# Lightning attention into a leaky-ReLU MLP on one core: another order of the first entries, and plan constants set for it

## Chip, core and metric

The kernel runs on one core of one Trainium2 chip. The metric is the device time of one execution in microseconds (us).

## What is computed

Block-wise linear attention with decay, for 4 batches, 8 heads, 768 tokens and head size 64, then a two-layer MLP on the 3072 tokens, all in float32 (the two weights arrive as float64).

```python
# attention, per block of 64 tokens; lam is one decay per head
intra = (q_b @ k_b^T * Dmask) @ v_b          # Dmask[i,j] = lam**(i-j) for i >= j
inter = (q_b * lam**(pos+1)) @ kv_state
out_b = intra + inter
kv_state = lam**64 * kv_state + (k_b * lam**(63-pos))^T @ v_b
# MLP: x is (3072, 512), w_in (512, 2048), w_out (2048, 512)
h = x @ w_in
out = maximum(0.01 * h, h) @ w_out
```

## The kernel before

**Tiles.** Tokens are worked in 24 chunks of 128 (c0 to c23; six to a batch, two blocks to a chunk) and 6 groups of four chunks. `w_in` is cut into 8 pairs of 256 columns each. To keep float32 accuracy on TensorE each operand is split into a head h, a low part l and a mixed part m; a product is three passes, xh·wh, xl·wl and xm·wm. Between the second and third pass ACT scales the PSUM bank (L658); after the third ACT applies the leaky ReLU and moves the bank out (L661, "evacuation"), and a DMA stores the result g to DRAM (L664).

**Entries.** The list `seq` names the work of the first two groups by hand: `a` (a whole chunk alone), `b` (load and transpose two chunks, scores of the first), `r` c (a chunk round: outputs of c, scores of c+1, transposes of c+2, loads of c+2), `wi` p (load and convert pair p of `w_in`), `up` g p (a unit: group g times pair p, or a part of its chunks), `ls`/`lt` (loads of many small pieces for later chunks). Later groups follow from a loop, and the second layer (`dl`, `dn`) comes at the end.

**The plan.** Each entry calls `add` with an engine, a cost, what it reads and writes, and the rank of its entry. `Plan.emit` runs a list schedule over those costs and issues the instructions in that order, so the order on each engine is fixed when the program is built: every engine works its own list strictly in turn. SP issues nearly all DMAs. A `busy` transposition (L266) fills gaps that the plan expects on PE.

**What a chunk does.** k and q (L338, two DMAs each) and v (L388) are loaded. PE transposes k and q (L403); for the first four chunks k goes to bank b11 (`KT`) and later to the upper half of `po`, q always goes to `pt`. ACT copies both to SBUF (L414 for k, L415 for q). POOL, or DVE for c < KM, scales k (L419). The q times powers of lambda (L423) is made by DVE straight from `pt` for c < QS, and else by POOL. PE makes scores and key-value products into `psc` (L313); DVE takes them out (L452 masked scores, L457/L459 state), POOL decays the state (L462). PE makes outputs into `po` (L313): own products, first inter products, then, after a tiny copy `seen_po` on ACT or DVE (L491), the second inter products. ACT writes xh (L507), DVE xl (L508) and xm (L510).

**What a weight pair does.** For each half: a load of float64 words into one of three `raw` buffers (L566, a "raw"), on ACT two conversions into `low` (L580, L582) and one into `w32` (L578), on DVE a shift and an add (L584, L585). Then the head wh on ACT or DVE (L591, L593), wl (L596) and wm (L602) on DVE. The three raw buffers, two `low` buffers and `w32` are used in turn by all pairs.

**Banks of the units.** Each unit has two blocks with a bank each. The first `EARLY` blocks alternate between b10 and b2; after that b10, b11 and b2 go round.

```python
kb = ("b10", "b2")[n_b % 2] if n_b < 0 else ("b10", "b11", "b2")[n_b % 3]   # n_b starts at -EARLY
```

**Constants that the change sets.** `LATER` is added to the rank of xm of the first group. `GOFIRST`: below it the scores of a chunk are issued before its key-value products. `SUBL`, `RUNS` and the costs in `load_kq` and `load_v` are costs and due times of loads in the plan. `SOON` is a table of latencies used for the fillers.

Of the kernel before, what the change touches and what calls it, by code (L numbers as in the profile page):

```python
# [31 lines left out]
def _bc(ap, idx, n):  # L32
    a = [list(x) for x in ap.ap]
    return bass.AP(ap.tensor, ap.offset, a[:idx] + [[0, n]] + a[idx:])


class Plan:

    LAG = {"PE": 0.25, "ACT": 0.1, "DVE": 0.1, "POOL": 0.12, "DMA": 3.5}
    SOON = dict(LAG, DMA=2.0)

    def __init__(self):
        self.ops, self.last, self.rank = [], {}, 0.0
# [36 lines left out]
    def emit(self):  # L83
        n = len(self.ops)
        follows, heads = {}, {}
        for c in self.chains.values():
            m = [i for i in c if "PE" in self.ops[i][0]]
            for i in c[1:]:
                self.ops[m[0]][2].update(self.ops[i][2] - set(c))
            heads[m[0]] = m[1:]  # L90
            follows.update((i, m[0]) for i in m[1:])
        locked = []
        left = [len(o[2]) for o in self.ops]
        users = [[] for _ in range(n)]
        for i, o in enumerate(self.ops):
            for d in o[2]:
                users[d].append(i)
        free = dict(self.first)
        ends = [[] for _ in range(n)]
        able = {e: set() for e in free}  # L100
        for i, o in enumerate(self.ops):
            if not left[i]:
                for e in o[0]:
                    able[e].add(i)

        def since(i, e):
            return max((t + (0.0 if e == x != "DMA" else self.LAG[x]) for t, x in ends[i]), default=0.0)

        def good(i, e, t):
            ways = self.ops[i][0]  # L110
            return all(t + ways[e] <= max(free[x], t) + ways[x] + 0.3 for x in ways)

        done = []
        while len(done) < n:
            best = None
            for e in free:
                for i in able[e]:
                    if e == "PE" and (i != locked[0] if locked else i in follows):
                        continue
                    t = max(free[e], since(i, e))  # L120
                    if (best is None or (t, self.ops[i][3]) < best[:2]) and good(i, e, t):
                        best = (t, self.ops[i][3], i, e)
            t, _, i, e = best
            ways, fn = self.ops[i][:2]
            if i in heads:
                locked = list(heads[i])
            elif locked and i == locked[0]:
                locked.pop(0)
            for x in ways:
                able[x].discard(i)  # L130
            us = ways[e]
            if e == "PE" and t < self.cold:
                us *= 1.5
            elif e == "DVE" and fn is not None and free["POOL"] > t:
                us += 0.4 * min(free["POOL"] - t, us)
            free[e] = t + us
            done.append((t, len(done), i, e))
            for u in users[i]:
                ends[u].append((free[e] + self.more.get(i, 0.0), e))
                left[u] -= 1  # L140
                if not left[u]:
                    for x in self.ops[u][0]:
                        able[x].add(u)
        self.timeline = sorted(done)

        soon = dict.fromkeys(free, 0.0)
        soon.update(PE=self.warm, DVE=self.first["DVE"], DMA=self.first["DMA"])
        over = [(0.0, None)] * n
        for t, _, i, e in self.timeline:
            ways, fn, deps = self.ops[i][:3]  # L150
            t = max([soon[e]] + [over[d][0] + (0.0 if over[d][1] == e != "DMA" else self.SOON[over[d][1]]) for d in deps])
            if e == "PE":
                if self.spare in self.ops[i][4]:
                    self.idle = None
                if self.idle is not None and t > soon[e] + 0.4:
                    self.idle(int((t - soon[e] - 0.2) / 0.22))
            soon[e] = t + ways[e]
            over[i] = (soon[e], e)
            fn() if len(ways) == 1 else fn(e)
# [3 lines left out]
def kernel(  # L163
# [10 lines left out]
    nc = tc.nc  # L174
    P = 128
    B, H, SEQ, D = q.shape
    C, C2 = P, P // 2
# [7 lines left out]
    NG = NCH // GC  # L185
    T = GC * C
    WARM = 11
    LATER = 5.0
    KT, EARLY = "b11", 2
    QS = 3  # L190
    KM = 1
    NRAW = 3
    TURN = 3
    SLACK, GSLACK = 4.0, 2.0
    EARLY_SLACK = 1.5
    GOFIRST = 2
    SUBL, FIRST = 0.75, -8.0

    DV = 10
    RUNS = {10: (-8.0, 0.8), 12: (4.0, 0.0)}  # L200
    C4 = P // 4
    HALF = (slice(0, D), slice(D, 2 * D))
    assert NCB % TURN == 0 and D == 64 and KO == HP == 4 and SEQ % C == 0 and NCH % GC == 0 and d_model == T == 512 and NP % 4 == 0
# [43 lines left out]
    kqv = [[x[:, i * H * D:(i + 1) * H * D].rearrange("p (h d) -> p h d", h=H) for i in range(2)] for x in kqv_f]  # L247
# [27 lines left out]
    def length(us, issue=0.5):  # L275

        return issue if steady else us

    def move(us, fn, reads, writes, issue=0.5, rank=0.0, slack=SLACK):

        plan.slack = slack if steady else EARLY_SLACK
        if steady and not rank:
            rank = FIRST
        add("DMA", length(us, issue), fn, reads, writes, rank=rank)
        plan.slack = 0.0
# [40 lines left out]
    def of(c):  # L326
        return c // NCB, c % NCB, c % 2
# [3 lines left out]
    def load_kq(c):  # L331
        b, n, i = of(c)
        for src, x, nm in ((k, 0, "k"), (q, 1, "q")):
            y, dst = src[b, :, n * C:(n + 1) * C, :], kqv[x][i]

            def go(y=y, dst=dst):
                for z in range(2):
                    nc.sync.dma_start(out=dst[:, z * HP:(z + 1) * HP, :], in_=y[z::2].rearrange("h p d -> p h d"))  # L338
            if nm == "k" or c < DV:
                move(1.15, go, [], [f"{nm}{i}"], issue=1.0)  # L340

    def run(c):

# [19 lines left out]
    def load_subs(c):  # L363
        b, n, i = of(c)
        count = run(c)[1]
        for nm, src, pieces in zip("kq", (k, q), subs(c, count)):
            for sub, lo, hi, keys in pieces:
                add("DVE", 0.0, lambda: None, [], keys)
                for y in range(lo, hi):
                    for a in range(4):  # L370
# [4 lines left out]
                                out=o.rearrange("j (m i) -> j m i", i=C4), in_=z.rearrange("(m j) i -> j m i", j=C4)),  # L375
                            keys, [f"{nm}s{y}{a}"], issue=SUBL, rank=RUNS.get(c, (4.0, 0.4))[0] + RUNS.get(c, (4.0, 0.4))[1] * (4 * y + a))

# [7 lines left out]

    def load_v(c):
        b, n, i = of(c)
        move(1.15, lambda: nc.sync.dma_start(out=kqv[2][i], in_=v[b, :, n * C:(n + 1) * C, :].rearrange("h p d -> p h d")),  # L388
            [], [f"v{i}"])

    def transposes(c):
# [17 lines left out]
        def copies():  # L409
# [3 lines left out]
            if c < DV:  # L413
# [3 lines left out]
            nr = slice(0, C2 if n == NCB - 1 else P)  # L417
            add(*((("DVE", "POOL"), (0.7, 1.1)) if c < KM else ("POOL", 1.1)),
                lambda e="POOL": ENG[e].tensor_tensor(kr[nr], kr[nr], _bc(pow_k, 3, D)[nr], op=ALU.mult), ["fk"], [f"k{i}"])  # L419
            m = slice(1 if n == 0 else 0, 2)  # L420
            o, x = (z.rearrange("p y (t i) -> p y t i", t=2)[:, :, m, :] for z in (qsTs[i], pt if c < QS else qTs[i]))
            eng, e, us, dep = ("DVE", nc.vector, 0.7, "pt") if c < QS else ("POOL", nc.gpsimd, 1.2, f"qT{i}")
            add(eng, us, lambda: e.tensor_tensor(o, x, _bc(pow_q, 2, 2)[:, :, m, :], op=ALU.mult), ["fq", dep], [f"qsT{i}"])  # L423
# [3 lines left out]
    def scores(c):  # L427
# [16 lines left out]

        if c < GOFIRST:
            add("PE", 0.47, go, [f"kT{i}", f"qT{i}"], ["psc"])
        add("PE", 0.47, kv, [f"k{i}", f"v{i}"], ["psc"])
        if c >= GOFIRST:
            add("PE", 0.47, go, [f"kT{i}", f"qT{i}"], ["psc"])
# [17 lines left out]
    def outputs(c, between=lambda: None):  # L467
# [38 lines left out]
        def uses():  # L506
# [3 lines left out]
            add("DVE", 0.7, lambda: nc.vector.scalar_tensor_tensor(xm, xl.bitcast(F32), -S, xh.bitcast(F32), op0=ALU.mult, op1=ALU.add),  # L510
                [h, l], [m], rank=LATER if c < GC else 0.0)

        return uses

    def alone(c):
        load_kq(c)
        load_v(c)
        transposes(c)()
        scores(c)()
        outputs(c)()  # L520

    def begun(c):

        for x in (c, c + 1):
            load_kq(x)
            load_v(x)
            transposes(x)()
        scores(c)()
# [159 lines left out]
    def down(g, p):  # L688

        nonlocal n_t  # L690
        for tb in range(GC):
# [43 lines left out]

    seq = [("a", 0), ("a", 1), ("a", 2), ("a", 3), ("b", 4), ("wi", 1), ("up", 0, 1), ("r", 4), ("wi", 0), ("r", 5),
# [4 lines left out]
    nxt, n_out, begin = 3 * GC, 0, len(seq)  # L743
    steps = [(g, p) for g in range(2, NG) for p in range(NP)]
    for n, (g, p) in enumerate(steps):
# [75 lines left out]
```

## Time and profile before

| | |
|---|---|
| median of 3 runs | 610.2 us (609.88 to 610.89) |
| profiled execution, its own time | 609.84 us |
| its span | 608.1 us |
| PE busy | 597.1 us, 98% of the span |
| DVE / ACT / POOL busy | 313.2 / 267.9 / 85.6 us |
| HBM read and written | 172 GB/s over the span |

The span is the time between the first and the last instruction in the trace; the execution's own time has the start and the end of the program in addition. Busy times are sums over instructions. PE's matmuls are pipelined, and their ends are modelled. In a timeline row the columns are start, duration, engine, line, operation, what it writes and reads, and, in brackets, the idle time before it and what released it.

### The profile page before, as it was taken

Reading aid. Unit: us, or ns where it says so; the run is one execution under the profiler, and the core shown is the slowest. Engines: PE = TensorE matmul, PEld = TensorE weight load, DVE = VectorE, ACT = ScalarE, POOL = GpSimd, SP = SyncE. Lnnn points to the kernel's source line nnn. Section 1 sums busy time; section 2 is a strip of 40 time slices with the busy share of each in tenths; the row PEclk is TensorE's granted clock in tenths of the full one; section 3 lists DMA queues with packets and bytes.
Section 4 is the critical chain, followed back from the end, with each engine's and each line's share of the span. In section 5 each row is a group of like instructions: output and inputs, shape, how many; then the busy total and the mean of one; then the engine's idle time right before and its main releaser. Section 6 shows DMA issues by size and latency. Waiting matters only on the chain.

```text
span 608.1 us, 12940 instructions
## 1 busy us (share of the span) xinstructions
PE 597.1 (98%) x5391; PEld 494.0 (81%) x5391; DVE 313.2 (52%) x417; ACT 267.9 (44%) x428; POOL 85.6 (14%) x91
## 2 busy tenths in 40 slices
PE   8799999999999999999999999999999999999997
PEld 6578888888888888888788888888888888888886
DVE  5899872334253426226366755545454544635531
ACT  4778874333455656565577422222222313214111
POOL 1653331215133014104000000000000000000000
PEclk9999999999999999999999999999999999999999
DMA  9899864767788888886686843424334343433201
GB/s 218 214 281 256 244 182 119 180 143 186 188 219 243 215 239 200 226 249 215 227 288 232 279 141 106 171 74 143 131 103 138 109 136 109 134 104 123 85 1 69
DMA packets 147754, 105.18 MB, mean 173 GB/s; under 512 B 123632, under 2 KB 124400, under 8 KB 147696
## 3 DMA queue, kind: packets, MB, share of 16 engines
q1 hardware_dynamic: 147552, 104.36, 58.9%
q8 instruction: 42, 0.69, 0.5%
q14 instruction: 16, 0.13, 0.1%
q10 hardware_dynamic: 144, 0.00, 0.0%
HBM read 68.69 MB, written 35.65 MB: 172 GB/s over the span
## 4 chain that ended last, share of the span: by engine, by line
PE 94%; DMA 2%; SPq 1%; ACT 1%; DVE 1%; issue 0%; DVEq 0%; ACTq 0%
PE b L640 44%; PE b L700 18%; PE po L700 11%; PE psc L700 11%; PE po L313 4%; PE pt L700 4%; PE psc L313 3%; DMA raw<-in_moe_w_in_dram 2%; SPq L338 1%; PE po L403 0%; PE pt L403 0%; ACT low L580 0%; DVE w L584 0%; DVE w L585 0%; SPq L388 0%
## 5 line engine op out<-in xcount | busy, mean ns | idle before, releaser
L682 ACT ACTIVATE xh<-att 128x1024 fp32r<-128x1024 f32 x48 | 50.7, 1060 | 148.9 <-PE b L700 140.7
L683 DVE SCALAR_TENSOR_TENSOR xl<-att,xh 128x1024 fp32r<-128x1024 f32 x48 | 58.6, 1222 | 95.6 <-ACT xh L682 95.6
L640 PE MATMUL b<-xh,wh 128*128 128x512 f32 (+1 forms) x392 | 102.9, 386 | 0.7 <-ACT xh L507 0.7
L640 PE MATMUL b<-xm,wm 128*128 128x512 f32 (+1 forms) x392 | 103.5, 391 | 0.0
L640 PE MATMUL b<-xl,wl 128*128 128x512 f32 (+1 forms) x392 | 102.8, 386 | 0.0
L640 PEld LDWEIGHTS b<-xh,wh 128*128 128x128 f32 x392 | 72.5, 188 | 15.8 <-ACT xh L507 0.9
L640 PEld LDWEIGHTS b<-xl,wl 128*128 128x128 f32 x392 | 72.5, 188 | 14.8
L658 ACT ACTIVATE b<-b 128x512 f32<-128x512 f32 x96 | 56.0, 584 | 63.1 <-PE b L640 63.1
L640 PEld LDWEIGHTS b<-xm,wm 128*128 128x128 f32 x392 | 70.9, 188 | 15.2 <-ACT b L658 0.7
L661 ACT ACTIVATE gs<-b 128x512 f32<-128x512 f32 x96 | 56.7, 598 | 42.2 <-PE b L640 37.7
L700 PE MATMUL b<-wh,xh 128*128 128x512 f32 x192 | 74.7, 389 | 0.0
L700 PE MATMUL b<-wl,xl 128*128 128x512 f32 x192 | 74.7, 389 | 0.0
L685 DVE SCALAR_TENSOR_TENSOR xm<-xl,xh 128x1024 fp32r<-128x1024 f32 x48 | 58.7, 1226 | 4.7
L700 PEld LDWEIGHTS b<-wl,xl 128*128 128x128 f32 x192 | 36.1, 188 | 7.6
L700 PEld LDWEIGHTS b<-wh,xh 128*128 128x128 f32 x192 | 36.0, 187 | 7.5
L452 DVE TENSOR_TENSOR att<-psc,att 128x512 f32<-128x512 f32 x24 | 16.5, 689 | 45.7 <-PE psc L313 45.7
L423 POOL TENSOR_TENSOR att<-att 128x512 f32<-128x512 f32 (+1 forms) x21 | 26.3, 1251 | 96.9 <-DVE att L383 42.5
L419 POOL TENSOR_TENSOR att<-att 128x512 f32<-128x512 f32 (+1 forms) x23 | 28.5, 1239 | 65.3 <-DMA att<-in_k_dram 19.9
L700 PE MATMUL psc<-wh,xh 128*128 128x512 f32 x96 | 37.3, 389 | 0.0
L700 PE MATMUL psc<-wl,xl 128*128 128x512 f32 x96 | 37.3, 389 | 0.0
L700 PE MATMUL psc<-wm,xm 128*128 128x512 f32 x96 | 37.3, 389 | 0.0
L700 PE MATMUL po<-wh,xh 128*128 128x512 f32 x96 | 37.3, 389 | 0.0
(73 smaller groups left out, 790.0 us busy)
## 6 DMA issues: line engine op xcount, KB each, us to landing
att<-g SPq DMA_DIRECT2D x48, 512.0 KB, 3.3
g<-gs SPq DMA_DIRECT2D x47, 512.0 KB, 4.0
raw<-in_moe_w_in_dram SPq DMA_DIRECT2D x16, 512.0 KB, 5.6
raw<-in_moe_w_out_dram SPq DMA_DIRECT2D x16, 512.0 KB, 4.7
att<-in_k_dram SPq DMA_DIRECT2D x48, 128.0 KB, 4.1
att<-in_v_dram SPq DMA_DIRECT2D x24, 256.0 KB, 4.3
out_dram<-gs SPq DMA_DIRECT2D x23, 256.0 KB, 2.1
wo<-w SPq DMA_DIRECT2D x8, 512.0 KB, 5.7
```

Source lines behind the costliest of these rows:

```text
L313: nc.tensor.matmul(dst[HALF[cols]], lhsT=lhsT[HALF[rows]], rhs=rhs[HALF[rows]], start=start, stop=True, skip_group_check=True)
L338: nc.sync.dma_start(out=dst[:, z * HP:(z + 1) * HP, :], in_=y[z::2].rearrange("h p d -> p h d"))
L419: lambda e="POOL": ENG[e].tensor_tensor(kr[nr], kr[nr], _bc(pow_k, 3, D)[nr], op=ALU.mult), ["fk"], [f"k{i}"])
L423: add(eng, us, lambda: e.tensor_tensor(o, x, _bc(pow_q, 2, 2)[:, :, m, :], op=ALU.mult), ["fq", dep], [f"qsT{i}"])
L452: add("DVE", 0.69, lambda: nc.vector.tensor_tensor(sc, psc[:, :, lower, :], decay, op=ALU.mult), ["psc", "fk"], ["sc"])
L640: nc.tensor.matmul(dst, lhsT=w[z][:, kk * 2 * P + f * P:kk * 2 * P + (f + 1) * P], rhs=x[z][:, kk, toks], start=start and kk == 0, stop=kk ...
L658: add("ACT", ns, lambda b=b: nc.scalar.activation(out=b, in_=b, func=AF.Copy, bias=0.0, scale=S + 1.0), [], [kb], rank=-1.5)
L661: add("ACT", ns, lambda b=b, r=r: nc.scalar.activation(out=r, in_=b, func=AF.Prelu, bias=0.0, scale=1.0 / WS, alpha=0.01), [kb], [f"gs{jg} ...
L682: add("ACT", 1.05, lambda: nc.scalar.activation(out=h, in_=graw[j], func=AF.Copy, bias=0.0, scale=NEAR), reads, wr("h"))
L683: add("DVE", 1.25, lambda: nc.vector.scalar_tensor_tensor(l, graw[j], 1.0, h.bitcast(F32), op0=ALU.mult, op1=ALU.subtract), reads + [f"rh{ ...
L685: add("DVE", 1.25, lambda: nc.vector.scalar_tensor_tensor(m, l.bitcast(F32), -S, h.bitcast(F32), op0=ALU.mult, op1=ALU.add), [f"rh{j}", f" ...
L700: nc.tensor.matmul(acc[tb][z // 2][:, cols], lhsT=ring[j][z][:, f * T + tb * P:f * T + (tb + 1) * P], rhs=W[pp][z][:, f * d_model:(f + 1) ...
```

## The change

The list `seq` for the first two groups is replaced. In the new list the second pair's `wi` 0 stays behind the first unit, and `wi` 2 and `wi` 3 follow it at once; the rounds of c4, c5 and c6 are named before the second unit; unit (0, 3) comes before the first part of (1, 1); the second part of (1, 1) comes before (0, 7); the rounds of c8 to c11 stand between other units of group 1; `ls` stands behind (0, 6). The constants are set anew. `SOON` moves from the class into `emit`, with the same values.

In the program that comes of it, the number of instructions on each engine stays nearly the same: PE has 41 fillers in place of 35; DVE makes five of the products L423 and POOL 19, in place of three and 21; `seen_po` is made by ACT 17 times and by DVE 7 times, in place of 16 and 8. The order changes on every engine.

```diff
-    SOON = dict(LAG, DMA=2.0)
...
+        SOON = dict(self.LAG, DMA=2.0)
...
-    LATER = 5.0
-    KT, EARLY = "b11", 2
-    QS = 3
-    KM = 1
+    LATER = 2.0
+    KT, EARLY = "b11", 4
+    QS = 5
+    KM = 4
...
-    GOFIRST = 2
-    SUBL, FIRST = 0.75, -8.0
+    GOFIRST = 3
+    SUBL, FIRST = 0.5, -8.0
...
-    RUNS = {10: (-8.0, 0.8), 12: (4.0, 0.0)}
+    RUNS = {10: (-6.0, 0.5), 12: (4.0, 0.0)}
...
-                move(1.15, go, [], [f"{nm}{i}"], issue=1.0)
+                move(1.3, go, [], [f"{nm}{i}"], issue=1.0)
...
-        move(1.15, lambda: nc.sync.dma_start(out=kqv[2][i], ...
+        move(1.0, lambda: nc.sync.dma_start(out=kqv[2][i], ...
...
-    seq = [("a", 0), ("a", 1), ("a", 2), ("a", 3), ("b", 4), ("wi", 1), ("up", 0, 1), ("r", 4), ("wi", 0), ("r", 5),
-           ("up", 0, 0), ("wi", 2), ("up", 0, 2), ("wi", 3), ("r", 6), ("wi", 4), ("wi", 7), ("up", 1, 1, 0, 2),
-           ("up", 0, 3), ("up", 0, 4), ("r", 7), ("wi", 6), ("up", 0, 7), ("up", 1, 7), ("wi", 5), ("up", 0, 6),
-           ("up", 0, 5), ("ls",), ("up", 1, 2), ("r", 8), ("lt",), ("up", 1, 0), ("up", 1, 3), ("r", 9), ("r", 10),
-           ("up", 1, 4), ("up", 1, 6), ("up", 1, 1, 2, 4), ("r", 11), ("up", 1, 5)]
+    seq = [("a", 0), ("a", 1), ("a", 2), ("a", 3), ("wi", 1), ("b", 4), ("up", 0, 1), ("wi", 0), ("wi", 2),
+           ("wi", 3), ("r", 4), ("r", 5), ("r", 6), ("up", 0, 0), ("up", 0, 2), ("r", 7), ("up", 0, 3), ("wi", 4),
+           ("up", 1, 1, 0, 2), ("up", 0, 4), ("wi", 7), ("up", 1, 1, 2, 4), ("up", 0, 7), ("wi", 6), ("wi", 5),
+           ("up", 0, 6), ("ls",), ("up", 1, 6), ("up", 0, 5), ("up", 1, 7), ("r", 8), ("lt",), ("up", 1, 3),
+           ("r", 9), ("r", 10), ("up", 1, 0), ("up", 1, 2), ("up", 1, 4), ("up", 1, 5), ("r", 11)]
```

More of the change, by code (lines that the diff above doesn't have):

```diff
@@ L150, in emit @@
             ways, fn, deps = self.ops[i][:3]
-            t = max([soon[e]] + [over[d][0] + (0.0 if over[d][1] == e != "DMA" else self.SOON[over[d][1]]) for d in deps])
+            t = max([soon[e]] + [over[d][0] + (0.0 if over[d][1] == e != "DMA" else SOON[over[d][1]]) for d in deps])
             if e == "PE":
@@ L387, in load_v @@
         b, n, i = of(c)
-        move(1.15, lambda: nc.sync.dma_start(out=kqv[2][i], in_=v[b, :, n * C:(n + 1) * C, :].rearrange("h p d -> p h d")),
+        move(1.0, lambda: nc.sync.dma_start(out=kqv[2][i], in_=v[b, :, n * C:(n + 1) * C, :].rearrange("h p d -> p h d")),
             [], [f"v{i}"])
```

## The prediction

> **What bounds the kernel now.** I read the page first, then busy time by windows, then the waits of PE, and last the timelines of PE, ACT and SP around the first unit (the first `up` entry). All chunks are numbered c0, c1, ...; a "pair" is one `w_in` entry.
>
> ```profile
> span 608.1 us, 12940 instructions
> PE 597.1 (98%) x5391; PEld 494.0 (81%) x5391; DVE 313.2 (52%) x417; ACT 267.9 (44%) x428; POOL 85.6 (14%) x91
> PE 94%; DMA 2%; SPq 1%; ACT 1%; DVE 1%; issue 0%; DVEq 0%; ACTq 0%
> ```
>
> The chain that ended last is PE for 94% of the span. Where does PE not work? The windows tell (columns: length, then busy time of PE, PEld, DVE, ACT, POOL, granted clock, DMA share, GB/s):
>
> ```profile
> 0.00:10.00 10.00, 8.30 (x110) 6.22 (x114) 4.96 (x21) 2.90 (x4) 1.14 (x8) 1.00 0.91 175
> 10.00:20.00 10.00, 7.91 (x262) 6.36 (x252) 7.73 (x15) 6.95 (x14) 4.59 (x6) 1.00 0.89 220
> 20.00:31.00 11.00, 7.76 (x219) 5.67 (x216) 9.34 (x14) 8.27 (x15) 8.43 (x8) 1.00 0.97 249
> 31.00:45.00 14.00, 14.00 (x164) 11.46 (x168) 13.38 (x18) 9.91 (x18) 6.62 (x6) 1.00 1.02 288
> 45.00:75.00 30.00, 30.00 (x470) 25.81 (x462) 27.71 (x38) 26.43 (x49) 12.11 (x11) 1.00 0.89 246
> 75.00:100.00 25.00, 25.00 (x230) 20.97 (x223) 13.39 (x17) 16.64 (x29) 5.48 (x5) 1.00 0.57 157
> 200.00:342.00 142.00, 141.72 (x1446) 117.16 (x1437) 68.72 (x102) 85.67 (x148) 19.23 (x21) 1.00 0.78 235
> ```
>
> Up to 31 us PE idles 7 us; from 31 us on there is no gap worth naming, and the clock is full throughout. So the time is: the start of the first unit (S), plus a block of matmuls that the change only reorders, plus the tail. The edit can win only before S, and lose only by opening a gap after S. From 31 to 75 us the three helpers are nearly as full as PE: DVE 27.71 of 30, ACT 26.43 of 30, the DMA engines 0.89 to 1.02. A new order can therefore cost there.
>
> **The change, step 1: before the first unit.** Same chunks, same two loads of pair 1. The SP list is unchanged up to v of c4. Now the end of c3 on ACT and on PE:
>
> ```profile
> 27.38 0.69 ACT L578 ACTIVATE w<-raw 128x512 f32<-128x512 f32 x1 [0.16 <-DMA raw<-in_moe_w_in_dram]
> 27.97 0.77 ACT L580 ACTIVATE low<-raw 128x512 uint16<-128x512 uint32 x1
> 28.60 0.14 ACT L491 COPY att<-po 128x2 f32<-128x2 f32 x1
> 28.63 0.80 ACT L582 ACTIVATE low<-raw 128x512 f16<-128x512 f32 x1
> 29.84 0.59 ACT L415 COPY att<-pt 128x512 f32<-128x512 f32 x1 [0.41 <-PE pt L403]
> 30.32 0.60 ACT L507 ACTIVATE xh<-po 128x512 fp32r<-128x512 f32 x1
> 28.86 0.88 PE L403 MATMUL pt<-att 128*128 128x128 f32 x4 [0.48 <-ACT att L491]
> 29.79 0.46 PE L313 MATMUL po<-att 64*64 64x64 f32 x16
> 30.98 2.12 PE L640 MATMUL b<-xh,wh 128*128 128x512 f32 x8 [0.73 <-ACT xh L507]
> ```
>
> S is set by ACT: a raw load lands, two conversions run, then the tiny `seen_po` copy at 28.60 releases PE; PE transposes q of c5, then does the last inter products of c3 (29.79 to 30.25); ACT copies xh (30.32), and the unit starts 0.66 us later. In the new order these inter products stand before the transposes, and ACT's copy of `pt` behind xh. So they start at 28.86 and end at 29.32, xh starts at 29.39 (ACT is free by about 29.3), and the unit can start at 30.05. The q transposes then fit between 29.32 and about 30.1. They now also wait for DVE, because with QS 5 the pow_q product of c4 reads `pt` on DVE. That costs DVE two products more, 0.69 us each, and POOL two fewer:
>
> ```profile
> 11.92 0.69 DVE L423 TENSOR_TENSOR att<-pt,att 128x512 f32<-128x512 f32 x1 [1.89 <-ACT att L415]
> 23.93 0.42 DVE L459 TENSOR_TENSOR att<-att,psc 128x256 f32<-128x256 f32 x1 [1.53 <-POOL att L462]
> 27.65 1.84 DVE L510 SCALAR_TENSOR_TENSOR xm<-xl,xh 128x512 fp32r<-128x512 f32 x2
> ```
>
> The product of c3 falls into DVE's idle 1.53 us before 23.93: nothing. The product of c4 takes the place of one of the two xm at 27.65 (0.92 each); the other one stands much earlier on DVE with LATER 2.0; 27.65 + 0.92 + 0.69 is 29.3, in time for the transposes. If DVE is late there, each 0.1 us late is 0.1 us on S. I take S = 30.1, a gain of 0.9 us; bounds 0.5 and 1.0, since the raw load at 27.38 holds `seen_po` in either order. An earlier disturbance I cost at nothing: q of c3 is now transposed before the scores of c2 and holds PE until it has landed, but k of c3 is issued after it and lands later still, and PE needs it next in both orders; the wait for k covers the wait for q, and if that cover fails the raw load at 27.38 still ends last. The six fillers more (41 for 35, L266) run in waits.
>
> **Step 2: the loads behind it.** With QS and LATER the SP list after v of c4 changes: raw, k of c5, raw, v of c5, raw, then q of c6 and c7. Before, q of c6 was first. SP rows, and then size and time from issue to landing of q of c6, v of c4, the raw at 30.37 and the first raw at 33.09 (k is loaded like q, in two pieces of 128 KB):
>
> ```profile
> 24.59 2.53 SPq L388 DMA_DIRECT2D att<-in_v_dram  x1
> 27.20 1.97 SPq L338 DMA_DIRECT2D att<-in_q_dram  x2
> 29.28 1.00 SPq L338 DMA_DIRECT2D att<-in_k_dram  x2
> 30.37 0.46 SPq L566 DMA_DIRECT2D raw<-in_moe_w_in_dram  x1
> 33.09 2.05 SPq L566 DMA_DIRECT2D raw<-in_moe_w_in_dram  x1
> ```
> ```profile
> att<-in_q_dram SPq DMA_DIRECT2D x2, 128.0 KB, 3.6
> att<-in_v_dram SPq DMA_DIRECT2D x1, 256.0 KB, 6.0
> raw<-in_moe_w_in_dram SPq DMA_DIRECT2D x1, 512.0 KB, 5.1
> raw<-in_moe_w_in_dram SPq DMA_DIRECT2D x1, 512.0 KB, 6.7
> ```
>
> So v landed at 30.6, the raws at 35.5 and 39.8. Between 30.6 and 39.8 there landed q, k, raw, v, q and raw, 2048 KB in 9.2 us: 0.45 us for 100 KB, in order of issue. In the new order the first raw (R1) is issued at 27.2: by its old 5.1 us it lands at 32.3, by the queue at 30.6 + 2.3 = 32.9. The second (R2) is issued near 28.7: by 6.7 us it lands at 35.4, by the queue at 32.9 + 3.45 = 36.3. I take the middles, R1 = 32.6 and R2 = 35.8. Both come about 3 to 4 us earlier than before. The question is who asks for them earlier still.
>
> The Trainium skill ("DMA: Bandwidth & Descriptors", Anatomy of one DMA) has a fit of 2.0 us plus bytes over 436 GB/s, made for descriptors built by GpSimd; by it, as an estimate, a raw takes 3.2 us. By that the raws would land at 30.4 and 31.9, no stall would follow, and the sum would be step 1 alone. The trace disagrees with 5.1 and 6.7 us.
>
> **Step 3: ACT's queue in front of PE.** In the new program ACT's order after xh is: copy of `pt`; the two low conversions of R1; copy of k of c4 out of `po`; scaling of b10; first low conversion of R2; scaling of b2; copy of k of c5; second conversion of R2; evacuation of b10 and b2. PE queues behind three of these: the k transposes of c5 need the copy of c4, the xm products need the scalings, and, with EARLY 4, the second unit's first block is b10 again instead of the free b11 and needs its evacuation. Before:
>
> ```profile
> 33.57 0.59 ACT L414 COPY att<-po 128x512 f32<-128x512 f32 x1 [2.64 <-PE po L403]
> 35.52 0.79 ACT L580 ACTIVATE low<-raw 128x512 uint16<-128x512 uint32 x1 [1.36 <-DMA raw<-in_moe_w_in_dram]
> 36.17 1.10 ACT L658 ACTIVATE b<-b 128x512 f32<-128x512 f32 x2
> 35.22 0.60 PE L403 MATMUL po<-att 128*128 128x128 f32 x4
> 36.84 2.12 PE L640 MATMUL b<-xm,wm 128*128 128x512 f32 x8
> 38.80 2.00 PE L640 MATMUL b<-xh,wh 128*128 128x512 f32 x8
> ```
>
> From S these PE steps come at +4.24 (k transposes), +5.86 (xm) and +7.82 (second unit). With S = 30.1: 34.3, 36.0, 37.9. ACT issues one conversion per 0.64 us (27.97 to 28.60), a scaling or evacuation per 0.55, a copy per 0.5 to 0.6. The copy of c4 is done at 32.6 + 0.64 + 0.64 + 0.6 = 34.5: stall 0.2. Then xm is at 36.2, its second half at 37.1, and the second unit would be at 38.1. From R2 on: 35.8 + 0.64 + 0.55 = 37.0, in time for the second half; + 0.5 (copy) + 0.64 + 0.55 = 38.7 for b10: stall 0.6. The second unit starts at 38.7, against 38.80. The gain of 0.9 is spent: -0.1 us, with bounds -0.6 (R1 32.3, R2 35.4) and +0.4 (R2 36.3).
>
> **Step 4: the later units.** PE reaches the fourth pair one round earlier, because the round of c5 (on PE from 52.95 to 55.94) now comes behind three groups of that unit:
>
> ```profile
> 51.50 0.69 DVE L593 TENSOR_SCALAR wh<-w 128x1024 fp32r<-128x1024 f32 x1
> 52.95 0.60 PE L403 MATMUL po<-att 128*128 128x128 f32 x4
> 55.94 1.19 PE L640 MATMUL b<-xh,wh 128*128 128x512 f32 x4
> ```
>
> DVE began the head of that pair at 51.5 and PE took it at 55.9, a margin of 3.7 us after the 0.69. The move takes the round's 3.0 us off it. But DVE comes to that head sooner too: masked scores and state of c5 now stand behind it. Following ACT's steps I estimate the head done at 51 to 52, with the need at 55.9 - 3.0 - 0.1 = 52.8. It holds, by about 1 us: zero, with up to 2 us if its loads slip. The units of group 1 and the sub-transfers (SUBL, RUNS) move behind 75 us, where DVE is at 13.39 of 25 and PE had no idle: zero. KM 4 leaves one k scaling on DVE as before, GOFIRST 3 lets the scores of c2 go before their keys are scaled, and the load costs 1.3 and 1.0 are numbers of the plan alone: what they do is in the orders above.
>
> **Sum.** The profiled execution took 609.84 us, of which 608.1 is the span. 609.84 - 0.1 is 609.7. The median of the three runs, 610.2, is 0.4 above the profiled execution, so I forecast 610.1. (About 0.2%, 1.2 us, is what a measurement of this kernel can tell from no change.)
>
> **The rivals.**
> - Loads are no limit: R2 lands by 34.6, ACT is free, and all of step 1 is kept: 610.2 - 0.9 = 609.3; with the upper bound of 1.0 and without the 0.3 us that PE lost between 30.98 and 36.84 beyond its own products, 608.9. For: the loads move up 3 us. Against: in the window to 31 us the DMA engines are at 0.97. Chance 0.25.
> - Slower, one mechanism: ACT blocked by R2. Each 0.1 us of R2 beyond 35.9 is 0.1 us at b10, and beyond 36.5 the scaling of b2 delays xm as well. If R2 lands at 37.5 to 38.5 (two more 256 KB loads served ahead of it, 1.15 us each), the second unit starts at 40.4 to 41.4: 1.6 to 2.6 slower, 611.8 to 612.8. For: ACT already waited 1.36 us for a raw at 35.52, in a place where it held nobody. Decides from R2 = 37. Chance 0.22.
> - Slower, supply: the fourth pair's head misses 52.8, or the pair after misses its own need; price 1 to 3 us, 611.2 to 613.2. For: DVE 27.71 of 30. Against: step 4. Chance 0.11. A miss needs the head 1 us later than I place it.
> - The plan's new numbers leave the order alone: excluded, the program's order differs on each engine.
>
> **How the numbers follow.** My forecast has 0.42, and stays within 0.2%. The first rival is faster by over 0.2% (below 609.0) in half of its chance, 0.13, else the same. The two slower ones hold 0.33, nearly all over 0.2%. So faster 0.13, same 0.54, slower 0.33. The range 608.9 to 612.6 leaves out some 0.1 on either side; that of the forecast alone is 609.5 to 610.7.
>
> **What would show it.** In the new profile: the first xh product at 30.1 (step 1); PE waiting for ACT at the k transposes of c5 and above all at the second unit's first product, with raw landings near 32.6 and 35.8 (steps 2, 3); no PE wait for DVE after 45 us (step 4). Wrong if PE starts its first unit after 30.6, if the second unit starts before 38.0 or after 39.5, or if a PE gap over 0.5 us stands anywhere later.

## The result

The changed kernel takes 618.11 us (median of six executions, 615.73 to 619.66) against 610.08 us (six executions, 609.66 to 610.89): a ratio of 1.0123, 95% interval 1.0103 to 1.0142. It is 1.2% slower, and the predicted range ended at 612.6. In the experiments further down the kernel before ran again beside each batch, with some executions near 613 us; a ratio compares whole sets of executions, so it can lie below the quotient of the medians. The profiled execution took 617.95 us, its span 616.2 us against 608.1. In the changed program every line number is one higher: L640 is now L641, L658 is L659, L661 is L662, L580 is L581, and so on.

**The start came as forecast.** PE's timeline of the changed kernel around the first two units:

```profile
29.11 0.46 PE L314 MATMUL po<-att 64*64 64x64 f32 x16 [0.86 <-ACT att L492]
30.30 2.12 PE L641 MATMUL b<-xh,wh 128*128 128x512 f32 x8
34.55 0.60 PE L404 MATMUL po<-att 128*128 128x128 f32 x4
36.17 2.12 PE L641 MATMUL b<-xm,wm 128*128 128x512 f32 x8
38.49 1.20 PE L641 MATMUL b<-xh,wh 128*128 128x512 f32 x4 [0.20 <-ACT gs L662]
```

The first unit starts 0.68 us earlier than before, the second 0.31 us earlier, with one short wait for an evacuation. PE then has no gap until 210 us.

**The loss stands at 212 and at 256 us.** These are the four largest of PE's ten rows of waits (columns: sum in us, times, longest):

```profile
PE b L641 <- ACT gs L662: 4.1, 2, 3.9
PE b L641 <- ACT b L659: 2.2, 1, 2.2
PE psc L314 <- DVE att L460: 1.7, 2, 1.1
PE b L267 <- POOL att L270: 1.4, 1, 1.4
```

The first two rows are new (the other two stand in the kernel before with 1.6 and 1.4 us); apart from the 0.2 us at 38.49 they come from two places in PE's timeline:

```profile
213.81 1.20 PE L641 MATMUL b<-xm,wm 128*128 128x512 f32 x4 [2.17 <-ACT b L659]
260.02 1.20 PE L641 MATMUL b<-xh,wh 128*128 128x512 f32 x4 [3.87 <-ACT gs L662]
261.05 1.73 PE L641 MATMUL b<-xm,wm 128*128 128x512 f32 x4
262.71 1.56 PE L314 MATMUL po<-att 64*64 64x64 f32 x48
```

PE waits for ACT's scaling and evacuation of its banks. Each takes ACT 0.6 us, as ever. ACT's own timeline shows what stood ahead of them (L581 and L579 are conversions of a half of `w_out`; `wo<-w` is the store of a converted pair, whose buffer L579 writes again):

```profile
209.69 0.79 ACT L581 ACTIVATE low<-raw 128x512 uint16<-128x512 uint32 x1 [1.91 <-DMA raw<-in_moe_w_out_dram]
210.35 0.76 ACT L583 ACTIVATE low<-raw 128x512 f16<-128x512 f32 x1
212.12 0.66 ACT L579 ACTIVATE w<-raw 128x512 f32<-128x512 f32 x1 [1.02 <-DMA wo<-w]
212.69 0.58 ACT L662 ACTIVATE gs<-b 128x512 f32<-128x512 f32 x1
...
256.04 0.78 ACT L581 ACTIVATE low<-raw 128x512 uint16<-128x512 uint32 x1 [3.81 <-DMA raw<-in_moe_w_out_dram]
256.69 0.75 ACT L583 ACTIVATE low<-raw 128x512 f16<-128x512 f32 x1
258.82 0.66 ACT L579 ACTIVATE w<-raw 128x512 f32<-128x512 f32 x1 [1.38 <-DMA wo<-w]
259.38 0.59 ACT L662 ACTIVATE gs<-b 128x512 f32<-128x512 f32 x1
```

ACT works its list in turn. Its conversion waits 1.91 and 3.81 us for a load of `w_out`, then 1.02 and 1.38 us for the store of the pair before, and the evacuations wait behind both. In the kernel before the first of these conversions started without a wait:

```profile
207.33 0.60 ACT L661 ACTIVATE gs<-b 128x512 f32<-128x512 f32 x1 [0.37 <-DMA att<-in_k_dram]
207.83 0.78 ACT L580 ACTIVATE low<-raw 128x512 uint16<-128x512 uint32 x1
```

The second did too, at 249.97. The load itself is not the slow part: from issue to landing the first took 4.9 us, in the kernel before 5.0, and the second 5.6 against 4.6. Why is it issued late? SP's queue, first before, then after. Each first row is the load ahead of the late one, and each second row the last small piece (48 KB) ahead of the late load; the rows between are 14 entries before and 20 after, small pieces and two stores of g:

```profile
190.55 0.42 SPq L569 DMA_DIRECT2D raw<-in_moe_w_out_dram  x1
...
199.97 0.56 SPq L374 DMA_DIRECT2D raw<-in_k_dram  x1
200.62 0.41 SPq L569 DMA_DIRECT2D raw<-in_moe_w_out_dram  x1
```
```profile
190.49 0.40 SPq L570 DMA_DIRECT2D raw<-in_moe_w_out_dram  x1
...
203.37 1.35 SPq L375 DMA_DIRECT2D att<-in_q_dram  x1
204.82 0.41 SPq L570 DMA_DIRECT2D raw<-in_moe_w_out_dram  x1
205.33 0.39 SPq L389 DMA_DIRECT2D att<-in_v_dram  x1
205.81 0.53 SPq L618 DMA_DIRECT2D wo<-w  x1
```

From load to load 10.07 us pass for 14 entries and 14.33 us for 20, so SP spends 0.72 us on each in both kernels, the load's own issue included. `SUBL` is what the plan believes of one: 0.5 us now, 0.75 before. With 0.5 the plan packs more pieces ahead of each load, and the load and the store behind it leave 4.2 us late. At the second place the load leaves at 250.40 after 243.09 before.

**The account.** The last matmul starts 8.12 us later (611.43 after 603.31). The two gaps are 2.17 + 3.87 = 6.04. Behind the second gap PE's clock fell (columns: length, busy time of PE, PEld, DVE, ACT and POOL, then the granted clock, DMA share, GB/s):

```profile
260.00:262.00 2.00, 1.98 (x7) 1.65 (x8) 1.97 (x5) 0.94 (x2) 0.49 (x1) 0.81 0.71 238
262.00:264.00 2.00, 2.00 (x50) 1.35 (x53) 0.35 (x1) 0.60 (x1) 0.79 (x1) 0.50 0.06 25
264.00:266.00 2.00, 2.00 (x94) 1.89 (x87) 0.49 (x1) 0.41 (x2) 0.21 (x1) 0.84 0.47 109
```

2.00 × (0.19 + 0.50 + 0.16) = 1.7 us of work were not done there. The start had left a gain of 0.15 at 201 us. 6.04 + 1.7 - 0.15 = 7.6 of 8.1. The rest lies in the gaps. The kernel a_nowo of the experiments, the changed one without the loads of `w_out`, has the same order on PE, so its matmuls can be set against these one by one. Ahead of the first gap the changed kernel is 0.49 us behind it, after that gap 2.96, after the second 7.12, and 8.65 once the clock is back at 266 us; at the end it is 8.60. So the gaps cost 2.5 and 4.2 us, some 0.3 more each than their rows show, and the clock 1.5: 8.2 in all, against 8.12 + 0.15.

### The profile page after: what moved, and what is told of

It reads as the page before. It is cut to its first block, busy times and chain, and to the rows that moved or that the text cites. A ratio compares the mean times of both kernels' runs of the same rounds, so it can differ in the third digit from the quotient of the medians.

```text
span 616.2 us, 12946 instructions
## 1 busy us (share of the span) xinstructions
PE 599.8 (97%) x5397; PEld 495.3 (80%) x5397; DVE 311.2 (51%) x418; ACT 269.3 (44%) x429; POOL 80.8 (13%) x89
## 4 chain that ended last, share of the span: by engine, by line
PE 91%; DMA 6%; ACT 1%; issue 1%; SPq 1%; DVE 0%; DVEq 0%; ACTq 0%
PE b L641 41%; PE b L701 18%; PE po L701 11%; PE psc L701 11%; PE po L314 4%; PE pt L701 4%; PE psc L314 3%; DMA raw<-in_moe_w_in_dram 3%; DMA wo<-w 2%; DMA att<-in_q_dram 1%; PE pt L404 0%; ACT gs L662 0%; ACT low L581 0%; PE po L404 0%; SPq L339 0%
## 5 line engine op out<-in xcount | busy, mean ns | idle before, releaser
L683 ACT ACTIVATE xh<-att 128x1024 fp32r<-128x1024 f32 x48 | 50.9, 1061 | 147.1 <-PE b L701 145.3
L641 PE MATMUL b<-xh,wh 128*128 128x512 f32 (+1 forms) x392 | 103.8, 387 | 4.2 <-ACT gs L662 4.1
L641 PE MATMUL b<-xm,wm 128*128 128x512 f32 (+1 forms) x392 | 104.5, 393 | 2.2 <-ACT b L659 2.2
L641 PE MATMUL b<-xl,wl 128*128 128x512 f32 (+1 forms) x392 | 103.2, 386 | 0.0
L641 PEld LDWEIGHTS b<-xh,wh 128*128 128x128 f32 x392 | 72.3, 188 | 20.9 <-ACT gs L662 5.5
L641 PEld LDWEIGHTS b<-xm,wm 128*128 128x128 f32 x392 | 71.2, 189 | 17.4 <-ACT b L659 2.8
L641 PEld LDWEIGHTS b<-xl,wl 128*128 128x128 f32 x392 | 72.5, 188 | 14.7
L659 ACT ACTIVATE b<-b 128x512 f32<-128x512 f32 x96 | 55.7, 583 | 56.2 <-PE b L641 56.0
L662 ACT ACTIVATE gs<-b 128x512 f32<-128x512 f32 x96 | 56.9, 596 | 48.5 <-PE b L641 45.1
L463 POOL TENSOR_TENSOR att<-att 128x256 f32<-128x256 f32 x40 | 31.3, 782 | 57.9 <-DVE att L460 56.3
L701 PE MATMUL po<-wl,xl 128*128 128x512 f32 x96 | 37.3, 389 | 0.0
```

The costliest lines, as they stand in the source:

```text
L463: add("POOL", 0.7, lambda new=new, j=j: nc.gpsimd.tensor_tensor(state[(j + 1) % 4], new, _bc(lam_c, 2, D), op=ALU.mult), [f"st{j % 4}", "f ...
L641: nc.tensor.matmul(dst, lhsT=w[z][:, kk * 2 * P + f * P:kk * 2 * P + (f + 1) * P], rhs=x[z][:, kk, toks], start=start and kk == 0, stop=kk ...
L659: add("ACT", ns, lambda b=b: nc.scalar.activation(out=b, in_=b, func=AF.Copy, bias=0.0, scale=S + 1.0), [], [kb], rank=-1.5)
L662: add("ACT", ns, lambda b=b, r=r: nc.scalar.activation(out=r, in_=b, func=AF.Prelu, bias=0.0, scale=1.0 / WS, alpha=0.01), [kb], [f"gs{jg} ...
L683: add("ACT", 1.05, lambda: nc.scalar.activation(out=h, in_=graw[j], func=AF.Copy, bias=0.0, scale=NEAR), reads, wr("h"))
L701: nc.tensor.matmul(acc[tb][z // 2][:, cols], lhsT=ring[j][z][:, f * T + tb * P:f * T + (tb + 1) * P], rhs=W[pp][z][:, f * d_model:(f + 1) ...
```

## The experiments

The theory: SUBL alone costs the 8 us, by the chain SP's queue, late `w_out` load, ACT standing, evacuations late, PE standing. Rivals: ACT's own new order, late small pieces, a load that is late because the DMA engines are full, and the new list itself. Kernels named a_ start from the changed kernel, those named b_ from the kernel before; each batch ran beside the kernel before (medians 610.39, 610.19 and 610.30 us).

**One constant, back and forth.**

```diff
a_subl75:  -SUBL, FIRST = 0.5, -8.0    +SUBL, FIRST = 0.75, -8.0
b_subl50:  -SUBL, FIRST = 0.75, -8.0   +SUBL, FIRST = 0.5, -8.0
a_subl60:  -SUBL, FIRST = 0.5, -8.0    +SUBL, FIRST = 0.6, -8.0
```

> The changed kernel with SUBL back at 0.75, all else new. Theory (SUBL alone loses the time: at a planned 0.5 us the plan puts 20 and 21 small pieces between two w_out loads on SP where it had 14 and 15 before; a piece takes about 0.65 us on the mean, so the load is issued 4 us late, ACT waits for it in front of a bank's evacuation, and PE behind ACT): PE's two waits of 2.2 and 3.9 us behind 200 us are gone, and 609.2 to 610.4 us, that is before less the 0.3 us that the second unit starts earlier. Rival 1 (the new list or another constant shifts the steady part): both waits stay, 616 to 619. Rival 2 (half and half): 611 to 615.

> The kernel before with SUBL 0.5 alone. Theory: 20 and 20 pieces between the same w_out loads, the same two waits of PE for ACT near 210 and 257 us of 2 to 4 us each, 614 to 619 us. Rival 1 (list or other constants): 610, no such wait.

> The changed kernel with SUBL 0.6. There are 17 and 18 pieces between those w_out loads. Theory: a load is late by 3 pieces instead of 6, some 2 us less than in the changed kernel; the first wait (2.2 us) gone or nearly, the second (3.9 us) 1.5 to 2.5 us, 610.5 to 614 us. A rival in which the order as such matters and not the number of pieces: no dose, 616 to 619 or 610.

| kernel | median, us | ratio, 95% interval | DMAs that SP issues between two `w_out` loads, most (from the third load on; a row x2 counts as two) |
|---|---|---|---|
| changed | 618.11 | 1.0123 (1.0103 to 1.0142) | 21 |
| a_subl75 | 610.49 | 0.9993 (0.9977 to 1.0008) | 16 |
| b_subl50 | 618.64 | 1.0121 (1.0084 to 1.0158) | 20 |
| a_subl60 | 612.20 | 1.0022 (1.0001 to 1.0042) | 18 |

One number carries the whole loss. In the traces the changed kernel and a_subl75 have the same order on every engine up to 182 us (then SP's differs, that of ACT and DVE from 200 us, that of PE from 211 us), so nothing in the start can be the cause. The kernel before counts 16 by the last column. a_subl75 lies 0.1 us above its expected range, b_subl50 within its own. With 0.75 the rest of the change is worth nothing that can be measured; with 0.5 the old list loses what the new one lost, and in the same way. b_subl50, PE's gaps and ACT's waits ahead of them:

```profile
214.34 1.19 PE L640 MATMUL b<-xh,wh 128*128 128x512 f32 x4 [2.03 <-ACT gs L661]
259.56 1.90 PE L640 MATMUL b<-xm,wm 128*128 128x512 f32 x4 [2.14 <-ACT b L658]
```
```profile
210.88 0.79 ACT L580 ACTIVATE low<-raw 128x512 uint16<-128x512 uint32 x1 [2.41 <-DMA raw<-in_moe_w_out_dram]
...
257.64 0.78 ACT L580 ACTIVATE low<-raw 128x512 uint16<-128x512 uint32 x1 [3.23 <-DMA raw<-in_moe_w_out_dram]
```

In a_subl75 the load leaves at 200.32 and ACT converts without a wait:

```profile
207.74 0.78 ACT L581 ACTIVATE low<-raw 128x512 uint16<-128x512 uint32 x1
208.38 0.77 ACT L583 ACTIVATE low<-raw 128x512 f16<-128x512 f32 x1
209.01 0.64 ACT L579 ACTIVATE w<-raw 128x512 f32<-128x512 f32 x1
```

a_subl60 lies between: PE waits 0.34 us at 213.24 and 0.58 us at 256.16, where 1.5 to 2.5 had been expected. The first unit of its profiled execution came at 31.75, though the order up to there is that of the changed kernel, so not all of that execution's time is SUBL's.

**More room in the plan for the load.** The plan adds a slack to a load's landing before it places what reads it:

```diff
-        move(1.6, get, after, [f"raw{j}"])
+        move(1.6, get, after, [f"raw{j}"], slack=9.0 if kind == "wo" else SLACK)
```

> The changed kernel with SUBL 0.5 kept, but the plan lets the conversions of a w_out load come 9 us behind the load instead of 4. Theory (what stops PE is that ACT, in order, stands at a conversion whose load is late, in front of an evacuation): the conversions stand later on ACT, behind more evacuations; ACT no longer holds PE, waits of PE behind 200 us under 1 us in all, 608.5 to 611.5 us, though SP is packed as densely. Rival (SP's queue as such: stores of g late, buffers gs not free): waits of 4 us or more stay, 614 to 619 us. Should the last w_out piece come so late that the second layer waits for it, a PE wait near 340 us would show that.

Measured: 670.16 us (ratio 1.0964). The expectation was badly missed, though the two waits at 210 and 257 us are gone: between 200 and 345 us PE waits for no scaling and no evacuation, and 1.9 us for `seen_po`. But the last load of `w_out` leaves at 380.79 us, where the changed kernel issues it at 324.77: the conversions run into the second layer, and three times there an xh (L683) comes late (waits of PE, the longest row):

```profile
PE psc L701 <- ACT xh L683: 40.5, 3, 13.7
```

Here the slack did not move the load forward; it moved the reader back.

**No load, and the load from another queue.**

```diff
a_nowo:  -move(1.6, get, after, [f"raw{j}"])
         +move(1.6, get if kind == "wi" else (lambda: None), after, [f"raw{j}"])
a_pool:  -nc.sync.dma_start(out=r64, in_=moe_w_out[...])
         +nc.gpsimd.dma_start(out=r64, in_=moe_w_out[...])
```

> The changed kernel without the sixteen loads of w_out (its conversions read what the buffer held before, so the second product's weights are not those of the reference); every other instruction stands where it stood on its engine. Theory (ACT, in order, stood behind a w_out load that SP issued 4 to 7 us late, and the evacuations behind it held TensorE): no wait of TensorE for ACT over 0.5 us behind 31 us, the clock at 1.00 in 260 to 266 us, 609.0 to 610.8 us. Rival 1 (the new order of the evacuations on ACT itself): waits of 2 us at 212 to 214 and of 4 us at 256 to 260 stay, 616 to 618. Rival 2 (the burst of small pieces on SP makes the pieces themselves late): the waits move to the transposes and scores, 612 to 616.

> The changed kernel with the same sixteen w_out loads issued from POOL's queue and not from SP's; nothing else changed. Theory (the place in SP's queue made the load late): the loads of 205 and 250 us are issued by 201 and 246, TensorE waits for ACT under 1 us in all behind 200 us, 609.0 to 611.0. Rival (the load is late because 16 DMA engines are full in the burst, 1.05 to 1.17 of busy share at 210 to 214 us, wherever it is issued): it lands as late as before, waits of 1.5 to 4 us stay, 613 to 618.

a_nowo: 610.17 us, ratio 0.9989 (0.9970 to 1.0009), no wait of PE for ACT over 0.3 us behind 31 us. Every other instruction keeps its place on its engine, so ACT's own order (rival 1) falls: it is the load. Late small pieces (rival 2) fall by the changed kernel's own trace, in which PE waits behind 45 us for nothing but ACT's two and, for 0.3 us, a `seen_po`. The run also shows that, with everything else as it is, no better order of these loads could gain anything that can be measured: without them the time is that of the kernel before.

a_pool: 613.06 us, ratio 1.0047 (1.0027 to 1.0067). The loads leave at 200.81 and 244.10, and ACT's wait for the load is gone, so the place in SP's queue made it late. Two things are left, so 609 to 611 was missed. First, the store of the pair before is still on SP and still late:

```profile
209.66 0.76 ACT L583 ACTIVATE low<-raw 128x512 f16<-128x512 f32 x1
212.17 0.66 ACT L579 ACTIVATE w<-raw 128x512 f32<-128x512 f32 x1 [1.75 <-DMA wo<-w]
```

Second, the load now runs beside the small pieces. DVE begins the turning of a set at 172.25 in the changed kernel and at 175.06 here, though SP issued that set no later, and PE waits 0.95 us for it. A piece of 48 KB issued between 163 and 171 us took 3.9 to 4.1 us to land by the median, in the changed kernel 2.5 to 2.8:

```profile
172.25 0.77 DVE L384 STREAM_TRANSPOSE att<-raw 128x256 f32<-128x256 f32 x2 [4.05 <-DMA att<-in_q_dram]
```
```profile
175.06 0.77 DVE L384 STREAM_TRANSPOSE att<-raw 128x256 f32<-128x256 f32 x2 [6.71 <-DMA g<-gs]
...
176.48 0.69 PE L314 MATMUL psc<-att 64*64 64x64 f32 x32 [0.95 <-DVE att L384]
```

The Trainium skill ("DMA: Bandwidth & Descriptors", Issuing engines are not separate DMA queues) says that transfers started by different engines run on the same 16 DMA engines and interleave, and that a second issuer saves only issue time. The rows agree: 4.0 us of issue saved at 200.81, 2.8 us of landing lost at 175.06.

**The store from POOL as well.**

```diff
a_poolwo = a_pool and
-            move(1.5, lambda: nc.sync.dma_start(out=WO[p], in_=w32f), ...)
+            move(1.5, lambda: nc.gpsimd.dma_start(out=WO[p], in_=w32f), ...)
```

> The changed kernel with the w_out loads and the stores of the wo pairs both issued from POOL's queue; nothing else changed. Theory (with the load early, what ACT still waits for at 209 to 212 us is the store of the pair before, issued late behind the same pieces on SP: 1.75 us, and TensorE 0.89): that wait of TensorE falls under 0.4 us, 610.0 to 612.3 us. Rival (POOL, in order, then holds the turning of k behind a store that waits for DVE): new waits of 0.5 us or more on transposes or scores, 612.5 to 616.

Measured: 613.52 us, ratio 1.0050 (1.0027 to 1.0073), above the expected range. The wait of 0.89 us at 213.85 is gone, as the theory has it; the wait for the turned pieces grows to 1.69 us at 177.44. Nothing is won: the loss has moved from the queue to the landing of the pieces. The rival named POOL standing behind a store; the trace shows the pieces landing late instead.

**The list alone, and the banks.**

```diff
b_seq:   the kernel before with the new seq, all constants kept
a75_e2:  a_subl75 and  -KT, EARLY = "b11", 4   +KT, EARLY = "b11", 2
```

> The kernel before with the new list of entries alone, all constants kept. Theory (the list of the first two groups costs nothing later, because the order of SP behind 75 us is the one of before; all the loss is SUBL's): 609.3 to 610.8, no wait of TensorE for ACT over 0.5 us behind 75 us. Rival (the list needs its constants: unit four or its weights late in the start): 611 to 613 with TensorE idle by 1 to 2 us more ahead of 75 us.

> The changed kernel with SUBL back at 0.75 and EARLY back at 2, which gives SP between the w_out loads the same numbers of entries as before the change. Theory: 609.3 to 610.8, as with SUBL 0.75 alone; the first unit at 30.3 to 31, no wait for ACT over 0.5 us behind 75 us. Rival (the rotation of the banks set by EARLY 4 is what holds the start's second to fourth unit together): TensorE waits for an evacuation by 0.5 to 1.5 us more ahead of 75 us, 611 to 612.

b_seq: 612.53 us, ratio 1.0023 (1.0002 to 1.0044), barely clear of no change; the time and the 1.2 us ahead of 75 us are those of its rival. The first unit of its profiled execution starts at 31.75 us, PE waits 1.2 us for xm (L510) between there and 75 us, and 0.73 us for an evacuation at 142.88. So the list alone seems not to be free, and to need the constants that came with it; one profile and an interval that nearly holds 1 do not show more. a75_e2: 611.35 us, ratio 1.0011 (0.9992 to 1.0030); one wait of 0.77 us for a scaling at 81.87 that a_subl75 doesn't have, which the theory excluded and the rival put ahead of 75 us. The interval does not settle whether EARLY 4 is worth that.

**The other end of SUBL.**

```diff
a_subl85, a_subl100:  -SUBL, FIRST = 0.5, -8.0   +SUBL, FIRST = 0.85, -8.0  /  1.0, -8.0
```

> The changed kernel with SUBL 1.0: SP between two w_out loads has at most 12 entries of small pieces, where 0.5 has 20, 0.6 18 and 0.75 15. Theory (only a burst of 18 and more makes a load so late that TensorE waits): no wait for ACT over 0.5 us behind 75 us, 609.3 to 611.0, like 0.75. Rival (each us of planned time for a piece spreads the conversions of w_out towards the end of the layer, and the last of its weights come late at 330 to 345 us): TensorE waits behind 300 us, 611.5 to 616.

> The changed kernel with SUBL 0.85: at most 14 entries between two w_out loads. Theory: no wait for ACT over 0.5 us behind 75 us and the early first unit kept, 609.2 to 610.8. Rival (as for 1.0, the conversions come late at the end of the layer): 611 to 614.

Measured: a_subl85 612.17 us, ratio 1.0028 (1.0012 to 1.0044), and a_subl100 621.97 us, ratio 1.0189 (1.0166 to 1.0213); both theories were missed. With fewer DMAs between the `w_out` loads (at most 15 and 13) PE waits 0.7 us at most for a scaling or evacuation behind 75 us, but other things come too late. With 1.0, PE:

```profile
250.71 1.99 PE L314 MATMUL psc<-att 64*64 64x64 f32 x64 [3.88 <-DMA att<-in_v_dram]
253.84 3.68 PE L641 MATMUL b<-xh,wh 128*128 128x512 f32 x8 [0.71 <-ACT xh L508]
```

My rival had a loss, but put it at 330 to 345 us and into the conversions; it is the load of v at 250 us. It was issued at 243.40, behind a load and a store of 512 KB, and took 7.2 us to land. Why it took that long stays open, and so does the loss of a_subl85. What is shown is that the constant has a narrow best place in this kernel: 618 at 0.5, 612 at 0.6, 610.5 at 0.75, 612 at 0.85, 622 at 1.0. The best of these is near the 0.72 us that an entry took on SP.

## Why the prediction was wrong

**Steps 1 to 3 held.** First unit: 30.1 forecast, 30.30 measured. Raw R1: 32.6, against the 31.96 at which ACT took it; R2: 35.8, against 35.53. Second unit: 38.7, measured 38.49 with the wait that step 3 placed at b10's evacuation (0.6 forecast, 0.20 measured); the wait of 0.2 at the k transposes did not come. The gain of step 1 (0.9 forecast, 0.68 measured) and the stalls of step 3 (0.8 forecast; the second unit starts 8.19 us after the first, against 7.82 before, so 0.37) were both too big and offset each other. That the times fit to 0.2 us is luck in part. Eight of the kernels here (the changed one, a_subl75, a_subl60, a_subl85, a_subl100, a_nowo, a_pool, a_poolwo) have the same order on every engine up to 158 us, and in their profiles the first unit starts at 29.76 to 31.75 and the second at 38.00 to 39.74; the kernel before and b_subl50, alike up to 184 us, start the first at 30.98 and 31.50. The first rival (nothing waits for the loads) and the second (blocked by R2, which needed R2 at 37) both fell.

**Step 4, first half, held.** The fourth pair starts without a wait, at 52.68 for a need placed at 52.8:

```profile
52.68 1.08 PE L641 MATMUL b<-xh,wh 128*128 128x512 f32 x4
```

a_subl75 agrees with the sum of all this: without SUBL's effect the change is at 0.9993, where -0.1 us had been forecast. Its interval, 1.4 us below the kernel before to 0.5 us above it, is too wide to show more.

**The step that failed** is one sentence in step 4: "The units of group 1 and the sub-transfers (SUBL, RUNS) move behind 75 us, where DVE is at 13.39 of 25 and PE had no idle: zero." It had three faults. It named DVE as the cover, but what SUBL moves stands on SP, and the prediction shows no row of SP's queue behind 75 us. It read free time on an engine as room for delay, but ACT, idle for 56 us of 142 there, is blocked by its order and not by its load. And it costed SUBL as a number of the plan, without asking what lies behind the moved entries on their queue: a `w_out` load about every 10 us, which the next conversion on ACT needs. The kernel before already showed what was needed: 14 entries in 10.07 us are 0.72 us each, so by estimate a plan that counts 0.5 gives away 20 × 0.22 = 4.4 us by the twentieth; the load left 4.2 us late. The term put at zero measured 8 us: 6.0 us of gaps by their rows, 6.6 when set against a_nowo, and the clock.

The mechanism itself was in the prediction, one stage too early. The second rival was ACT in order behind a late raw, with PE waiting for the evacuation. It was priced for `w_in` at 36 us and not asked for `w_out` at 210 us. The point that was to show the prediction wrong, a gap of PE over 0.5 us anywhere later, is what happened.

**The clock** was in no term of the sum. By the windows it added 1.7 us to 6.0 us of gaps.

## What to carry over

A planner's cost for an entry on a queue is a claim about the queue: before changing it, take the queue's rows between two dependent transfers, divide the time by the number of entries, and compare. When a change moves small transfers, look at the large one behind them, at who reads it, and at what stands behind that reader on an engine that works in order. An engine's share of idle time says nothing of how long it may be held up.

## What the runs showed of the chip

Gaps of 2 us on PE can cost more than their length. In b_subl50 gaps of 2.03 and 2.14 us were each followed by a clock of 0.50 (columns as above; the fourth row stands behind the second gap):

```profile
214.00:216.00 2.00, 1.66 (x6) 1.40 (x7) 1.78 (x2) 1.25 (x3) 1.06 (x1) 0.86 1.05 222
216.00:218.00 2.00, 2.00 (x6) 1.52 (x6) 1.54 (x4) 0.60 (x1) 0.04 (x1) 0.50 0.82 164
218.00:220.00 2.00, 2.00 (x19) 1.35 (x21) 0.41 (x1) 0.69 (x2) 0.70 (x1) 0.79 0.86 342
260.00:262.00 2.00, 2.00 (x6) 1.61 (x5) 0.72 (x2) 1.45 (x3) 0.00 (x0) 0.50 0.58 213
```

2.00 × (0.14 + 0.50 + 0.21) = 1.7 us of work were not done behind the first. In a_subl100 the gap of 3.88 us at 250.71 was followed by up to twice that, 2.00 × (0.39 + 0.50 + 0.50 + 0.32) = 3.4 us, of which PE idled some:

```profile
250.00:252.00 2.00, 1.29 (x48) 1.32 (x52) 0.38 (x1) 0.00 (x0) 0.51 (x1) 0.61 0.81 275
252.00:254.00 2.00, 1.29 (x45) 1.10 (x37) 0.87 (x2) 0.60 (x1) 0.55 (x1) 0.50 0.72 120
254.00:256.00 2.00, 2.00 (x5) 1.62 (x6) 1.53 (x3) 0.00 (x0) 0.29 (x1) 0.50 0.27 44
256.00:258.00 2.00, 2.00 (x7) 1.59 (x7) 0.42 (x1) 0.00 (x0) 0.96 (x2) 0.68 0.84 212
```

In the changed kernel the gap of 2.17 us at 213.81 was followed by full clock, and the one of 3.87 us was not. The six executions of the changed kernel fit a cost that comes in steps, and not in every execution, by their mean clock: spans of 613.9 us at 0.999, 615.4 and 616.2 at 0.997, and 616.5 to 617.9 at 0.994 (means 613.9, 615.8 and 617.3). The Trainium skill ("TensorE: Matmul & The Clock Gate", What's actually happening) has the clock halved after at least one idle window of about 3.4 us. The 3.87 us agree; the 2.03 and 2.14 us are shorter than that and halved it too. In a sum for this kernel a gap from 2 us on can therefore carry nothing more, 1.7 us, or up to 3.4 us; what decides between them these runs do not show.
